# An attention and feed-forward kernel whose order of operations is held as a table

## The chip, the core and the metric

One core of a Trainium2 chip runs the program. Its engines are PE (TensorE, matmuls), DVE (VectorE), ACT (ScalarE), POOL (GpSimd) and SP (SyncE, which here only issues DMAs). Each engine runs its own instructions in their order and waits for the others by semaphores. The metric is the device time of one execution in microseconds (us), lower is better; three runs of the kernel before gave 217.38, 217.80 and 217.99.

## The reference

Attention over four batches of 8 heads, 768 positions and 64 dimensions, in which a position sees the first four positions (the sinks) and the last 128; its output, 3072 rows of 512, goes through a feed-forward layer with 2048 hidden units and a squared relu.

```python
def _attn_ref(q, k, v, n_sink, window):
    B, H, S, D = q.shape                      # 4, 8, 768, 64
    scores = 1.0 / np.sqrt(D) * np.matmul(q, k.transpose(0, 1, 3, 2))
    pos = np.arange(S)
    rel = pos[:, None] - pos[None, :]
    keep = (pos[None, :] < n_sink) | ((rel >= 0) & (rel < window))   # 4, 128
    scores = np.where(keep, scores, -1000000000.0)
    scores = scores - np.max(scores, axis=-1, keepdims=True)
    a = np.exp(scores)
    a = a / (np.sum(a, axis=-1, keepdims=True) + 1e-09)
    return np.matmul(a, v)

def _moe_ref(x, w_in, w_out):                 # x: 3072 x 512, d_ff 2048
    r = np.maximum(x @ w_in, 0.0)
    return (r * r) @ w_out
```

## The kernel before

The kernel builds a list of 825 operations, each a Python closure that emits one or a few instructions, and then runs a planner over the list that fixes the order in which they are emitted and, for operations that more than one engine can do, the engine. As every engine runs what it was given in order, this order is the schedule.

**Work.** For each batch b (0 to 3) and each pair of 128-row blocks s (0 to 2): q and k come in by DMA and are turned so that the head dimension lies on partitions. In batches 0 and 1 PE does it (`transpose`, tile `pt`, L708) and DVE or ACT copy the result out (`unload`, L402, L400); in batches 2 and 3 SP's transposing DMAs do. `scores` (L815, tile `ps`) multiplies two heads at once in two tiles of 64 rows by 128 columns of the array; `sink_scores` (L774, tile `pk`) uses tiles of 128 by 32, and its keys are copied together by `sink_keys` on DVE (L750). All other matmuls use the full 128 by 128. ACT takes the exponential (`expo`, L836), DVE or POOL the mask (`domask`, DVE L845 and L848, POOL L426, two instructions on POOL), PE the product with v (`values`, L884, tile `po`), DVE the division (`norm`, L900 and L901). The result is turned again for the feed-forward layer (`bridge`, L933, with a copy to `xT`, or a transposing DMA).

The first layer (`layer1`, L965, tile `pm`) is 16 matmuls of 256 columns or 8 of 512 for each operation, followed by `relu` (ACT L976 or DVE L978) and `square` (DVE L987 or ACT L985). In batch 3 it is replaced by a scheme with fewer products on sums of blocks (`layer1_fast`): a *quad* has seven products of 4 matmuls of 256 columns or 8 of 128 (L1085, names 1 to 7, in the order 1, 2, 5, 4, 3, 6, 7), and between them DVE takes differences (L1126), ACT or DVE a copy (`first`), a relu (L1141) and DVE a second relu with a sum (`final`, L1153); the squares are L1107 and L1109. Each difference must end before a later product of the quad may write the same half of the bank. Two quads belong to rows 0 to 255 (quads 0,0 and 0,1), four to the rest (1,0 to 1,3).

The second layer (`layer2`, L1174, tile `py`) uses 64 matmuls of 512 columns for two of batch 0's pairs; all other pairs of blocks u use `layer2_fast`: four sums on DVE (`sum`, L1242), seven products of 8 matmuls of 256 columns (L1284, in the order c, d, a, b, c, d, a), evictions between them (`x`, `u`: L400, L402, L1309, L1325, L1332) and the store of 256 rows by 512, 512 KB, from SP (L1359). The very last pair (batch 3, u=2, the `tail`) stores its quarters separately; its last product has 16 matmuls of 128 columns, and its two halves are copied by DVE and by ACT and stored by SP (L1352) and ACT (L1353).

**PSUM.** Two pools of two slots each, `att` and `den`, hold all matmul results. A slot is free again when its last reader is done; an operation that needs a slot waits for that, and so do all behind it on PE.

**The order.** `Plan.run` picks, again and again, the ready operation with the earliest start by assumed costs of each operation on each engine; two numbers for each operation (`SHIFTS`) move its start and its rank. `warm` puts matmuls of the identity into PE's early gaps.

**Names.** An operation's number is its place in the list. Used below: 319 and 325 are first-layer operations of batch 1; 210 the sink scores of batch 1; 341 a relu; 441 the first product of batch 1's second layer and 467 a later one, for which 459 makes a sum on DVE; 446 the eviction `u` of batch 1's pair 0; 407 a mask of batch 2; 616 the first product of pair 0 of batch 2's second layer, 624 and 646 products of its pairs 0 and 1; 683, 685 and 686 the products 5, 4 and 3 of quad 0,0; 743, 721 and 760 products of quads 1,2, 1,0 and 1,3; 779 a product of batch 3's pair 0; 801 the last product of batch 3's pair 1, 802 to 804 its last sum, its first quarter and its 512 KB store; 820 the tail's last product, 822 the copies and stores of its two halves; 39 a load of batch 1's keys.

Of the kernel before, what the change touches and what calls it, by code (L numbers as in the profile page):

```python
# [17 lines left out]
LATENCY = 0.135  # L18
PE_SLACK = 0.0
DMA_START = {"sp": 1.45, "act": 1.2, "pool": 1.6}  # L20
DMA_LATENCY = 0.9
WARM_UNTIL = 34.0
SHIFTS = {
    None: ((-0.254, -0.2), (-0.571, -0.26), (-3.153, 0.8), (-0.345, -0.74), (-0.83, 3.28), (-0.98, -0.76),
        (1.458, 1.69), (-1.232, 0), (0.55, -0.13), (-1.841, -0.16), (-0.527, -1.31), (-1.271, -0.72), (-0.963, 0.32),
        (0.605, -2.77), (-1.323, 1.3), (-1.6, 0.58), (-2.678, -2.44), (-1.476, -0.28), (-2.561, -0.7),
        (-1.331, -0.42), (-1.151, -0.2), (-1.253, -0.22), (-0.398, -0.87), (0.902, 2.55), (-1.318, -0.7),
        (-1.389, -0.4), (-1.246, -0.74), (-0.947, 8.2), (-1.272, 0.2), (-0.428, -2.57), (-1.738, 0), (-1.257, -0.22),
        (-0.151, -1.78), (0.73, -2.69), (-1.258, -0.08), (-1.109, 1), (-1.269, -0.18), (-0.332, -1.95),
        (-1.198, 0.88), (-1.403, -0.28), (-0.085, 0.43), (-1.257, -0.22), (-1.492, -0.14), (-1.966, -0.82),  # L30
        (-1.228, 2.28), (-0.609, -0.3), (-1.172, -0.72), (-0.948, 1.33), (-1.214, -0.14), (-0.818, 0.07),
        (0.509, 0.34), (-1.258, 0.66), (-1.614, 0.1), (-0.282, -0.76), (-0.521, -1.37),),
    ('prep', 0, 0): ((-0.212, 1.23), (-0.072, -0.24), (-0.19, 0.16), (-0.726, 0.34), (0.102, 1.1), (-0.535, 0.02),
        (-0.602, -0.59), (0.354, 0.3), (-3.718, -4.59), (0.634, 0.85), (-0.293, -1.06), (-1.346, -1.52),
        (-0.272, 0.1), (0.418, -0.32), (-0.151, 0.16), (-0.447, -0.7), (0.314, -0.72), (0.319, 0.77), (-0.551, 0.09),
        (-0.072, 0.2), (-0.13, 0.16), (0.105, 0.24), (1.083, 0.83), (0.872, 0.89), (-0.583, 0.42), (-0.732, -0.4),),
    ('sink', 0, 0): ((4.752, 1.43), (1.667, 2.03),),
    ('att', 0, 0): ((0.347, 0.31), (0.954, 0.9), (-0.499, -1.83), (0.762, -2.15), (0.932, -0.05), (-2.305, -7.94),
        (-0.09, 0.64), (-0.608, -0.19),),
    ('val', 0, 0): ((-0.669, 0.31), (-0.697, -0.27), (2.439, -2.91), (-0.554, 0.35), (-0.437, -0.15), (-0.471, 0.35),  # L40
        (-0.386, 0.35), (-0.377, 0.25),),
    ('turn', 0, 0): ((1.726, 0.79), (1.562, 0.69), (1.948, 1.13), (1.496, 0.73),),
    ('att', 0, 1): ((3.244, 0.46), (11.783, 1.08), (3.403, 0.48), (2.622, -0.1), (0.081, -0.49), (-0.044, -0.15),
        (11.287, 1.58), (1.317, -0.32), (2.357, -0.58), (1.537, 1.18), (-0.135, 0.19), (-0.111, -0.81),),
    ('val', 0, 1): ((-1.139, 2.3), (-0.295, 1.56), (-0.887, 1.68), (-0.625, 1.18), (-3.257, -5.22), (-3.374, -3.06),
        (-3.291, -3.92), (-2.551, -2.62),),
    ('turn', 0, 1): ((0.396, -1.51), (-0.815, -0.63), (-0.017, -0.23), (-0.694, 0.15), (-0.252, 1.39),),
    ('prep', 0, 1): ((0.244, -0.3), (0.839, 0.68), (-0.246, 0.32), (0.932, -0.62), (1.027, -0.56), (0.209, -0.32),),
    ('sink', 0, 1): ((1.975, -1.87), (0.782, -1.52),),
    ('att', 0, 2): ((0.244, -0.66), (-1.989, 0.29), (-0.493, 0.33), (0.159, -0.68), (1.032, 0.54), (0.796, 0.57),  # L50
        (-0.189, 0.02), (1.388, -0.12), (0.48, -0.01), (0.313, -0.14), (1.032, 0.72), (-1.933, -0.09),),
    ('val', 0, 2): ((-0.074, -1.39), (-0.782, 0.91), (-0.843, -3.97), (-0.333, 0.47),),
    ('turn', 0, 2): ((0.672, -0.31), (-0.118, -0.09), (0.809, -0.71), (2.596, 0.84),),
    ('l1', 0, 0): ((1.946, 1.98), (2.477, 2.05), (2.842, 0.55), (1.744, 2.15), (1.004, -3.64), (-0.401, 3.09),
        (1.762, -0.33), (2.032, -0.69), (0.818, -0.26), (0.463, 0.08), (2.529, 0.93), (3.08, -0.59),),
    ('l1', 0, 1): ((-1.505, -0.48), (0.385, 0.7), (-1.5, -0.46), (0.416, -0.68), (-0.498, 0.3), (-0.582, 0.6),
        (-0.46, -0.02), (-0.566, -0.1), (0.513, -0.12), (-0.444, -0.02), (-1.914, 1.12), (-0.022, 0.42),),
    ('l1', 0, 2): ((1.159, -0.13), (1.171, -0.31), (4.523, 0.49), (0.77, -0.87), (1.53, -0.41), (0.926, -0.79),
        (0.522, -0.76), (1.124, -0.01), (1.066, -0.47), (4.319, 0.45), (0.749, -2.99), (0.301, -1.88),),
    ('prep', 1, 0): ((-3.284, 0.24), (-1.096, -0.94), (0.605, -0.58), (0.247, -2.12), (-5.483, 0.49), (0.694, 0.02),  # L60
        (0.597, -0.24), (0.597, -0.24), (-8.208, 1.17), (0.681, -1.4), (-1.5, -0.64), (0.357, -0.54), (-10.29, 0.97),
        (0.494, -0.72), (0.633, -0.24), (-0.776, -0.16), (0.529, -0.04), (-1.768, -0.84),),
    ('sink', 1, 0): ((0.868, 0.19), (0.763, 0.03),),
    ('att', 1, 0): ((-0.287, -0.2), (-4.964, -0.65), (-1.435, -0.81), (-3.607, -0.91), (-2.001, -0.01),
        (-0.447, -0.1), (-0.674, 0.1), (-0.719, -0.6), (-0.604, 0.18), (-0.781, -0.2),),
    ('val', 1, 0): ((-6.954, 1.31), (0.072, -4.26), (-0.107, -0.44), (-0.058, -0.46),),
    ('turn', 1, 0): ((-4.522, 0.82), (-0.734, 2.5), (-1.073, 0.44), (0.276, 0.05),),
    ('att', 1, 1): ((1.003, 0.22), (1.223, 0.6), (0.413, -0.45), (0.232, -0.07), (0.259, -0.21), (0.322, -0.07),
        (1.914, -1.56), (0.055, 0.01), (0.085, -2.03), (0.176, 0.47),),
    ('val', 1, 1): ((0.205, 0.29), (-0.249, -0.53), (-2.761, 0.71), (0.377, -0.27),),  # L70
    ('turn', 1, 1): ((0.754, 1.22), (2.068, -0.78), (0.857, 1.68), (-4.788, 1.81),),
    ('prep', 1, 1): ((2.397, 1.96), (5.859, 1.94), (-0.449, 1.75), (1.83, 1.58), (1.97, 1.7), (0.173, -0.21),),
    ('sink', 1, 1): ((0.987, -0.02), (-0.036, -5.62),),
    ('att', 1, 2): ((1.119, -4.28), (0.959, -0.36), (0.499, 1.02), (0.438, -0.34), (1.738, -0.38), (0.767, 0.25),
        (1.547, -0.3), (1.332, 0.31), (1.014, 0.54), (0.269, -2.08),),
    ('val', 1, 2): ((1.128, -0.41), (3.047, 0.37), (3.469, 0.88), (2.416, -3.47),),
    ('turn', 1, 2): ((-4.356, -7.65), (-0.607, -0.19), (-1.006, 0.46), (-4.587, -4.53),),
    ('wt', 0): ((-0.423, 0.42), (-0.315, 0.14), (-1.716, 1), (-0.361, 0.06),),
    ('l2', 0, 0): ((6.071, 1.48), (1.943, -1.23), (2.592, 0.39), (0.401, -1.21), (5.784, 0.74), (5.992, 1.58),
        (2.993, -2.81), (2.732, 0.86), (0.489, -0.39), (-0.516, -1.21), (2.415, 0.45),),  # L80
    ('l2', 0, 1): ((-0.438, 1.25), (-0.215, 0.46), (-0.282, 0.35), (0.307, -0.75), (-0.329, 0.71), (0.749, -0.74),
        (0.871, 0.46), (0.785, 0.08), (0.702, 1.69), (-0.352, 0.8), (2.254, -2.28),),
    ('sum', 0, 2): ((0.045, -1.68), (0.204, -1.02), (-0.718, -2.55), (0.064, -1.38),),
    ('l2', 0, 2): ((0.177, 0.43), (0.08, 0.05), (0.043, -0.01), (0.087, 0.13), (0.146, -0.05), (0.286, 0.01),
        (-3.566, 0.64),),
    ('ev', 0, 2): ((0.387, -2.73), (0.215, -1.01), (-0.063, -1.45), (-0.129, -4.69), (0.419, -1.95), (0.228, -0.91),
        (-0.334, -3.43), (0.529, -0.75),),
    ('l1', 1, 0): ((-2.25, 1.33), (0.301, 1.9), (2.02, -1.38), (0.412, 0.1), (0.164, 0.26), (0.039, -0.22),
        (0.926, -8.17), (-0.524, 0.12), (0.373, 0.12), (1.304, 1.55), (1.015, 0), (0.579, -0.12), (0.204, -0.09),
        (0.523, 0.4), (-0.028, -0.17), (-1.901, 0.85), (0.353, 0.12), (0.196, 0.02), (-1.978, -2.11), (1.417, -0.02),  # L90
        (0.319, -0.99), (0.194, -4.07), (-3.291, 0.39), (0.291, 2.35),),
    ('l1', 1, 2): ((2.497, -0.43), (3.349, 0.01), (2.786, -0.17), (2.851, -0.17), (2.812, 1.03), (0.807, 1.08),
# [109 lines left out]
}  # L202


class Slot:

    def __init__(self, pools, readers):
        self.pools = (pools,) if isinstance(pools, str) else pools  # L210
        self.pool, self.readers, self.end = self.pools[0], readers, 0.0


class Op:
# [6 lines left out]

class Plan:

    def __init__(self, capacity):
# [8 lines left out]
    def place(self, shifts):  # L240

        seen = {}
# [1238 lines left out]
```

## Time and profile before

| | us |
|---|---|
| three runs | 217.38, 217.80, 217.99 (median 217.80) |
| the profiled execution | 217.69 |
| its span, first to last instruction | 216.0 |
| ACT, POOL busy in the span | 123.2, 98.7 |
| granted TensorE clock | 1.00 |

How to read it: a row of the timeline is start, length, engine, line, operation, output and inputs, shape, and how many instructions were merged; in brackets the idle time before it and what ended it. Matmuls overlap in a pipeline and their ends are modelled, so the distance between starts tells more than the lengths. Groups of instructions end in: total busy time, mean ns of one | idle time before them. Some of them, which carry prices below:

```profile
L976 ACT ACTIVATE r<-pm 128x1024 bf16<-128x1024 f32 x30 | 30.7, 1023 | 17.3 <-PE pm L965 15.6 <-DVE gT_sb L987 1.4
L978 DVE TENSOR_SCALAR r<-pm 128x1024 bf16<-128x1024 f32 x6 | 7.3, 1220 | 2.0 <-PE pm L965 2.0
L987 DVE TENSOR_TENSOR gT_sb<-r 128x1024 bf16<-128x1024 bf16 x26 | 19.3, 741 | 17.3 <-ACT r L976 17.1
L848 DVE TENSOR_TENSOR expm<-expm,tri 128x1024 bf16<-128x1024 bf16 x14 | 11.0, 791 | 5.1 <-ACT expm L836 4.9
L426 POOL TENSOR_SCALAR_AFFINE_SELECT expm<-expm 128x512 bf16<-128x512 bf16 x36 | 27.3, 787 | 55.9 <-ACT expm L836 43.7 <-DVE xn_sb L901 12.2
out_dram<-osb SPq DMA_DIRECT2D x11, 512.0 KB, 3.7
```

### The profile page before, as it was taken

How to read it: one execution, taken by the hardware profiler on the slowest of the kernel's cores; microseconds unless marked ns; L12 is line 12 of the kernel's file. 1: busy time of each engine (PE TensorE's matmuls, PEld its weight loads, DVE VectorE, ACT ScalarE, POOL GpSimd, SP SyncE). 2: the span in 40 equal slices, each digit the busy share in tenths (PEclk: the TensorE clock that was granted, in tenths of full speed). 3: DMA queues.
4: the chain of work that ended last, by engine and by line, in shares of the span. 5: the costliest groups of instructions: out<-in, count | busy, mean ns of one | idle time of the engine just before them, and what ended most of it. 6: DMA issues, size and time to landing. Idle time of an engine off the chain costs nothing.

```text
span 216.0 us, 5470 instructions
## 1 busy us (share of the span) xinstructions
PE 206.5 (96%) x2287; PEld 165.4 (77%) x2287; DVE 161.5 (75%) x292; ACT 123.2 (57%) x158; POOL 98.7 (46%) x137
## 2 busy tenths in 40 slices
PE   3999999999999999999999999999999998999993
PEld 3858996689486755688887965598898998897882
DVE  6487458773958569688689994477995859999973
ACT  2498567366663775976757268566623369482100
POOL 7799773698935974898954424002302000000000
PEclk9999999999999999999999999999999999999999
DMA  5999999999997699999999936000023260000133
GB/s 156 261 182 206 174 199 213 160 154 205 156 147 169 88 147 133 167 108 147 142 199 133 139 84 209 3 0 0 3 97 75 52 219 3 2 0 5 55 132 107
DMA packets 93625, 26.09 MB, mean 121 GB/s; under 512 B 86816, under 2 KB 91552, under 8 KB 93600
## 3 DMA queue, kind: packets, MB, share of 16 engines
q0 software_dynamic: 69248, 12.59, 80.3%
q1 hardware_dynamic: 24168, 13.07, 28.1%
q8 instruction: 18, 0.29, 0.6%
q10 hardware_dynamic: 184, 0.07, 0.1%
q14 instruction: 7, 0.06, 0.1%
HBM read 27.30 MB, written 6.29 MB: 156 GB/s over the span
## 4 chain that ended last, share of the span: by engine, by line
PE 73%; DVE 14%; ACT 3%; DMA 3%; issue 3%; SPq 2%; DVEq 0%; ACTq 0%
PE pm L965 29%; PE py L1284 20%; PE po L884 6%; PE py L1174 6%; PE ps L815 5%; PE pm L1085 4%; DMA qr<-in_q_dram 3%; DVE sg L1242 3%; ACT expm L836 2%; DVE t L1126 2%; DVE r L1153 2%; SPq L557 2%; PE px L933 1%; DVE gT_sb L1109 1%; DVE expm L848 1%
## 5 line engine op out<-in xcount | busy, mean ns | idle before, releaser
L965 PE MATMUL pm<-xT,w_in_sb 128*128 128x256 bf16 (+1 forms) x448 | 66.1, 304 | 0.0
L965 PEld LDWEIGHTS <-w_in_sb 128*128 128x128 bf16 x448 | 48.3, 114 | 13.4 <-issue 1.3
L836 ACT ACTIVATE expm<-ps 128x1024 bf16<-128x1024 f32 (+1 forms) x48 | 43.7, 951 | 18.1 <-PE ps L815 17.5
L426 POOL TENSOR_SCALAR_AFFINE_SELECT expm<-expm 128x512 bf16<-128x512 bf16 x36 | 27.3, 787 | 55.9 <-ACT expm L836 43.7
L976 ACT ACTIVATE r<-pm 128x1024 bf16<-128x1024 f32 x30 | 30.7, 1023 | 17.3 <-PE pm L965 15.6
L1284 PEld LDWEIGHTS <-gT_sb 128*128 128x128 bf16 x336 | 31.2, 98 | 4.3 <-issue 0.7
L987 DVE TENSOR_TENSOR gT_sb<-r 128x1024 bf16<-128x1024 bf16 x26 | 19.3, 741 | 17.3 <-ACT r L976 17.1
L1284 PEld LDWEIGHTS <-sg 128*128 128x128 bf16 x240 | 22.4, 98 | 4.5 <-DVE sg L1242 1.0
L1284 PE MATMUL py<-wt,sg 128*128 128x256 bf16 x160 | 20.8, 273 | 0.4 <-DVE sg L1242 0.4
L1284 PE MATMUL py<-wt,gT_sb 128*128 128x256 bf16 x160 | 20.8, 273 | 0.0
L1284 PE MATMUL py<-w_out_sb,gT_sb 128*128 128x256 bf16 x144 | 18.5, 273 | 0.0
L884 PEld LDWEIGHTS <-expm 128*128 128x128 bf16 x352 | 16.3, 97 | 2.5 <-issue 0.7
L901 DVE TENSOR_TENSOR xn_sb<-po,rc 128x512 bf16<-128x512 f32 (+1 forms) x28 | 17.2, 615 | 1.0
L884 PE MATMUL po<-v,expm 128*128 128x65 bf16 x352 | 17.5, 193 | 0.3 <-DVE xT L402 0.2
L1174 PE MATMUL py<-w_out_sb,gT_sb 128*128 128x512 bf16 x64 | 15.3, 380 | 0.0
L848 DVE TENSOR_TENSOR expm<-expm,tri 128x1024 bf16<-128x1024 bf16 x14 | 11.0, 791 | 5.1 <-ACT expm L836 4.9
L815 PE MATMUL ps<-qkT 64*128 64x256 bf16 (+1 forms) x256 | 14.6, 238 | 0.0
L815 PEld LDWEIGHTS <-qkT 64*128 64x128 bf16 x256 | 8.1, 94 | 7.1 <-issue 6.1
L884 PE MATMUL po<-vs,es 128*128 128x65 bf16 x128 | 12.9, 193 | 0.0
L400 ACT ACTIVATE osb<-py 128x256 f32<-128x256 f32 (+1 forms) x15 | 6.6, 441 | 10.2 <-PE py L1284 7.1
L884 PEld LDWEIGHTS <-es 128*128 128x128 bf16 x128 | 11.7, 97 | 0.0
L587 POOL DMA_DIRECT2D v<-in_v_dram x12 | 11.0, 927 | 0.2
(97 smaller groups left out, 330.5 us busy)
## 6 DMA issues: line engine op xcount, KB each, us to landing
out_dram<-osb SPq DMA_DIRECT2D x11, 512.0 KB, 3.7
v<-in_v_dram POOLq DMA_DIRECT2D x24, 128.0 KB, 7.5
qn<-in_k_dram POOLq DMA_DIRECT2D x20, 128.0 KB, 7.5
qn<-in_q_dram POOLq DMA_DIRECT2D x20, 128.0 KB, 7.4
w_in_sb<-in_moe_w_in_dram POOLq DMA_DIRECT2D x4, 512.0 KB, 10.3
w_out_sb<-in_moe_w_out_dram POOLq DMA_DIRECT2D x4, 512.0 KB, 10.2
qr<-in_k_dram SPq DMA_DIRECT2D x4, 256.0 KB, 5.7
qr<-in_q_dram SPq DMA_DIRECT2D x4, 256.0 KB, 5.3
```

The lines of the kernel that those rows point to most:

```text
L426: nc.gpsimd.affine_select(out=e_tile, in_=e_tile, compare_op=ALU.is_ge, fill=fill, base=i - 1, pattern=[[0, n], [1 if i else -1, 128]], ch ...
L587: return [nc.gpsimd.dma_start(out=v_sb[b % 2][:, t, :, 0:D], in_=v[b, :, 128 * t:128 * t + 128, :].rearrange("h p d -> p h d"))]
L815: nc.tensor.matmul(ps[:, h2, o:o + w], lhsT=qkT_sb[r, m, 1, c, :], rhs=qkT_sb[r, m, 0, qb:qb + w // 128, :], start=(i == 0 and not biased) ...
L836: nc.scalar.activation(out=x[:, :, o:512], in_=bank_t["s", b, s, m][:, :, o:512], func=AF.Exp, scale=scale)
L848: nc.vector.tensor_mul(y, y, tri.rearrange("p (o a) c -> p o (a c)", o=1).to_broadcast([128, 4, 256]))
L884: touch(("po", b, s, m0), e, nc.tensor.matmul(pv[:, i, h2, :], lhsT=lhsT, rhs=rhs, start=(n_ == 0), stop=(n_ == len(mms) - 1)), j)
L901: touch(("po", b, s, m0), e, nc.vector.tensor_tensor(out=xn_sb[:, 2 * s:2 * s + 2, 128 * (m0 + j0):128 * (m0 + j0 + nj)].rearrange("p i (j ...
L965: nc.tensor.matmul(pm[:, i, :], lhsT=w_in_sb[:, fb // 4, kb, fb % 4:512:4], rhs=xT[:, c0 // 256:(c0 + cw) // 256, kb, :], start=(kb == 0), ...
L976: nc.scalar.activation(out=o, in_=h, func=AF.Relu)
L987: nc.vector.tensor_mul(g, r, r)
L1174: touch((b, u), e, nc.tensor.matmul(pm[:, i, :], lhsT=gT_sb[:, fb, 128 * t:128 * t + 128], rhs=w_out_sb[:, fb, :], start=(fb == 0), stop=( ...
L1284: ins = nc.tensor.matmul(y_, lhsT=x[:, i, :], rhs=r_, start=(first or tail and n == 2) and i == 0, stop=i == HB - 1, skip_group_check=not ...
```

## The change

The planner, its costs and the table `SHIFTS` go. A table `ORDER` lists the 825 operations in the order in which they are emitted. A letter behind a number names the engine where there is a choice (p, d, a, g for PE, DVE, ACT, POOL), and `+0` or `+1` which PSUM pool a slot is taken from. `DUMMIES` gives the number of identity matmuls before an operation. The operations are the same; 91 of them are on another engine than before.

```diff
-LATENCY = 0.135
-PE_SLACK = 0.0
...
-SHIFTS = {
...
+ORDER = """
...
+168 171 169d 159 172a 173d 160a 170a 165 131 177 166d 167d 178d 132a 133a 161a 144 146 145 148 174 128 289 149d 130d
...
+396 399 397 322 254+1 255 263+0+0 264 333a 339d 323d 324d 258g 371 372 260g 265d 340 261+0 398 262 341a 266 267d 319
...
+526a 640a 621a 520a 609 615 641 634 639 620 679+1 680 693+1 623 695a 694 697 642 681d 650 622 643 676 683 682 685
+624 651 696 698 677 625 678 646 644 594 595 610 611 684 686 699 687a 700 627 645 647 626 648d 652 689 690 701a 703
+654 691 628 707 692d 629a 704 655 739+0 657 740 688a 649 710 705 708 653 656a 741a 743 725+1 711+1 706a 702a 713a
+727a 659a 742 744 709 712 726 658 661 729 714 767 715 717 745 660 663 664 662 665 716 728 730 769 731 732 666 667d
...
+808 781 811a 810 812 813 816 783 787 815 817 784a 785 788 789 814d 790 791 792d 818 819 824 793 796 794 797 795d 821
+823 798 799 800 801 802 820 822 803a 804
+"""
+DUMMIES = {
+    57: 26, 63: 18, 64: 3, 83: 3, 91: 3, 97: 5, 101: 3, 119: 2,
 }
...
     def run(self):
-        free = {p: [0.0] * n for p, n in self.capacity.items()}
...
-                cand = (round(pick[1] + o.lag, 2), o.key)
-                if best is None or cand < best[0]:
-                    best = (cand, o, pick)
...
+        free = dict(self.capacity)
+        names = {"p": "pe", "d": "dve", "a": "act", "g": "pool"}
+        words = ORDER.split()
+        assert len(words) == len(self.ops)
+        for word in words:
+            word, *chosen = word.split("+")
+            n = int(word.rstrip("pdag"))
+            o = self.ops[n]
+            assert o.engine is None and all(a.engine for a in o.after + o.follow), n
+            o.engine = names[word[-1]] if word[-1] in names else next(iter(o.engines))
             for s in o.takes:
-                free[s.pool].sort()
-                free[s.pool].pop(0)
...
+                if len(s.pools) > 1:
+                    s.pool = s.pools[int(chosen.pop(0))]
+                assert free[s.pool], (n, s.pool)
+                free[s.pool] -= 1
+            self.idle = DUMMIES.get(n, 0)
+            o.run(o.engine)
             for s in o.reads:
                 s.readers -= 1
-                s.end = max(s.end, end)
                 if not s.readers:
-                    free[s.pool].append(s.end)
...
+                    free[s.pool] += 1
...
     def warm(dst, key=None, h=0):
-        if P.now < WARM_UNTIL:
-            for _ in range(min(26, int(0.5 * P.gap / 0.056))):
...
+        for _ in range(P.idle):
+            ins = nc.tensor.matmul(dst, lhsT=ident, rhs=ident, start=True, stop=True,
+                                   is_transpose=dst.dtype == BF16)
...
-    P.place(SHIFTS)
     P.run()
```

## The prediction, made before the changed kernel was run

> **What bounds the kernel now.** The page first: which engine is full, and what the chain that ended last runs through.
>
> ```profile
> PE 206.5 (96%) x2287; PEld 165.4 (77%) x2287; DVE 161.5 (75%) x292; ACT 123.2 (57%) x158; POOL 98.7 (46%) x137
> PE 73%; DVE 14%; ACT 3%; DMA 3%; issue 3%; SPq 2%; DVEq 0%; ACTq 0%
> ```
>
> PE is busy nearly always, so a new order of the same matmuls can only win where PE loses time inside that busy share. To find it I read the timeline of PE by starts, not by ends: with nothing in the way a matmul of 256 columns starts 109 ns after the last, one of 128 after 56, of 65 after 29, of 512 after 216. Whatever exceeds that is lost.
>
> ```profile
> 60.35 1.04 PE L1284 MATMUL py<-w_out_sb,gT_sb 128*128 128x256 bf16 x8
> 61.32 0.61 PE L815 MATMUL ps<-qkT 64*128 64x128 bf16 x12
> 61.87 1.05 PE L1284 MATMUL py<-wt,sg 128*128 128x256 bf16 x8
> ```
>
> Eight steps of 109 ns are 0.87 us, but the scores start 0.97 us after the product: 0.10 us for the change of tile from 128 to 64 rows; leaving costs about 0.09 more (148 ns for a 56 ns step). PE changes its tile shape 64 times, so 64 x 0.10 = 6.5 us go there. The other losses are waits:
>
> ```profile
> 176.67 0.61 PE L1085 MATMUL pm<-xs,w_in_sb 128*128 128x128 bf16 x8 [0.18 <-DVE t L1126]
> 178.39 1.05 PE L1085 MATMUL pm<-xs,wi 128*128 128x128 bf16 x16 [0.22 <-ACT r L1141]
> 179.93 1.06 PE L1085 MATMUL pm<-xs,qkT 128*128 128x256 bf16 x8 [0.48 <-DVE xs L1043]
> ...
> 199.81 0.61 PE L1284 MATMUL py<-wt,sg 128*128 128x256 bf16 x4 [0.38 <-DVE sg L1242]
> ```
>
> Here batch 3's fast first layer runs alone on PE while its sums and differences queue on DVE. By starts, PE loses 2.6 us between 172 and 193, 0.54 at 199.8 and 0.19 at 208.8; between 17 and 172 only 1.5 us in eight places. Together 4.8 us: all that a better order can take from waits.
>
> The windows view says who is full there:
>
> ```profile
> 172.00:193.00 21.00, 19.79 (x226) 18.69 (x224) 17.81 (x28) 14.34 (x18) 0.00 (x0) 1.00 0.19 63
> 193.00:200.00 7.00, 6.62 (x61) 5.72 (x60) 6.76 (x10) 2.94 (x5) 0.00 (x0) 1.00 0.01 4
> ```
>
> The columns are length, PE, PEld, DVE, ACT, POOL, clock: DVE is full from 193 to 200 (6.76 of 7.00), ACT is not. The clock is 1.00 throughout, so it is no lever.
>
> Last, the end, from the timeline:
>
> ```profile
> 208.41 0.38 SPq L1359 DMA_DIRECT2D out_dram<-osb  x1
> ...
> 212.48 0.28 ACT L400 ACTIVATE half<-ya 128x128 f32<-128x128 f32 x1 [3.32 <-PE ya L1284]
> 212.78 0.35 ACTq L1353 DMA_DIRECT2D out_dram<-half  x1
> 213.22 0.40 SPq L1352 DMA_DIRECT2D out_dram<-osb  x1
> ```
>
> The last matmul ends at 212.4, call it E. The 512 KB store of batch 3's second pair goes out at 208.41, well before; only quarters follow. The last, 64 KB at 213.22, lands 1.8 us later by the DMA view, and 0.95 us of closing work ends the span at 216.0 = E + 3.6.
>
> **The change, part by part.**
>
> *Planner gone, table in.* Host work; no instruction. The first 32 PE operations stand as before and the dummy matmuls are the same counts, so the start (to about 25 us) is priced at nothing; what follows keeps PE as its cover.
>
> *Shape changes.* I wrote PE's 260 operations out in both orders: blocks of scores or sink scores change the shape 64 times before, 63 after. One change fewer: -0.1 us. What the change says of tile shapes is done, and is worth almost nothing.
>
> *Engines.* 91 operations change engine. Up-projection relu: 13 to DVE, 4 back, 9 x 1.220 = +11.0 us of DVE; its squares: 7 to, 11 back, -4 x 0.741 = -3.0; masks: 7 from POOL, 3 back, +4 x 0.791 = +3.2; narrow evictions net 5 x 0.42 = +2.1; two 512-wide ones +1.3; batch 3's relu, spread and copy 1.22 + 0.74 + 0.64 = +2.6; its squares net -0.7; turns' copies -1.4. Sum +15.0 us on DVE (161.5 to about 176, 82% of the span); ACT loses 7.9, POOL 6.3. The cover is PE's own time: from the first layer-2 product of batch 1 (441) on, PE has 107 us of rows, DVE 107 by the mean durations and 102 by start-to-start steps (a DVE 0.69 follows the last after 0.61); before it was 97 by the means. Hidden, but with little left.
>
> *A rule against this.* Beside a POOL mask, DVE steps stretch:
>
> ```profile
> 147.67 0.98 DVE L1242 TENSOR_TENSOR sg<-gT_sb 128x1024 bf16<-128x1024 bf16 x1
> 148.69 0.69 DVE L1242 TENSOR_TENSOR gT_sb<-gT_sb 128x1024 bf16<-128x1024 bf16 x1
> ```
>
> POOL masks at 146.89 to 148.11, and the step beside it takes 0.98 for 0.69. The Trainium skill, "SBUF — State Buffer", section "Who interferes with whom", says that a DVE instruction with two SBUF inputs and a GpSimd one that reads SBUF exclude each other for a whole instruction. By that rule each of the 28 mask instructions left on POOL (36 before) could hold DVE for its whole 0.787 us, 22 us at worst. By the row it is 0.3 each, and only where they meet. My sum uses the row's means, which hold it.
>
> *PE's order in the middle (32 to 164).* I laid the operations out with the rows' durations: PE at its steps (product 0.87, sixteen 256-wide matmuls 1.75, scores 0.55 + 0.10, values 0.72), each relu, mask or norm behind its matmul in its engine's own order, each PSUM slot free when its last reader ends. PE then waits at few places. Sink scores of batch 1 (210): their keys stand behind a relu on DVE, 0.25. Up-projection 319 needs a "den" slot; the relu (341) that frees it stands behind a square on ACT, 0.5. Product 467 needs the sum 459, eighteenth in an unbroken row of DVE steps since 446 (11.0 us from 30.2 against PE at 40.9), 0.35. Some ten more are just in time or 0.1 late. Sum 1.8, against 1.5 before: no gain here.
>
> *Layer 2 of batch 2 spread through batch 3's first layer.* Quads 0,0 and 0,1 now start 13 PE places earlier, and thirteen products of 0.87 us stand between quad products that wait for each other. Example: 686 needs the difference of 683; before, nothing but quad products stood between. Now 624 and 646 do, 2 x 0.87 us, against a difference of 0.69 and its queue. Laid out the same way, about 0.7 us of waits remain from 616 on (743 behind ACT's queue 0.2, 721 0.25, 760 and 779 about 0.1 each) against 3.3 before: -2.6.
>
> *DMAs and queues.* POOL issues the same loads in the same order. A sink-values step (1.75 us) moves in front of 39, but these loads already sit behind landings ("POOL qn L578 <- DMA w_out_sb" waits 5.3 us), so it costs nothing. Batch 3's fourteen loads now go ahead of three masks: 14 x 0.9 = 12.6 us, and mask 407 is needed 9 us after. Of SP, the transposes change places among themselves and have 4 us or more to spare.
>
> *The end.* The order of batch 3's pairs is now 0, 2, 1, with pair 2's last quarter at the very end. So the 512 KB store (804) is last. Its first quarter (803) is moved to ACT, behind 822 in ACT's order, and 822 waits for the last matmul: 0.28 copy and 0.35 issue, then 0.38 for 803, so 804 goes out at about E + 1.1 where the last 64 KB went at E + 0.8. It moves 512 KB: the store of 208.41 ran at 254 to 264 GB/s from 209 to 211, done 2.7 us after its issue; the page's median is 3.7. I take 2.8: E + 3.9, and 0.95 to close gives E + 4.9 for E + 3.6: +1.3 us (bounds +0.9 and +2.2).
>
> *Sum.* -0.1 + 0.3 - 2.6 + 1.3 = -1.1 us against the profiled 217.69: 216.6. The runs' median, 217.8, lies 0.1 above that execution: **216.7**, which I forecast. The bounds: waits from 616 on may all go (-3.3) or stay (0), the middle may cost nothing (-1.5) or 2 us more than laid out.
>
> **The rivals.**
>
> *DVE becomes the bound (slower).* From 441 on DVE has 102 us of steps and PE 107 + 2; I count some 3 us in which DVE must itself wait for PE. That leaves 4 us. If DVE's steps take their full means there (107), 5% more, each unbroken row of some 11 us like that before 467 ends 0.55 us later; five such rows make 2.7 us more waiting, of which I take 2.5: 216.7 + 2.5 = 219.2. For it: DVE is the engine that ends PE's waits now, and gets 10 us more. Against: before, its steps did overlap. It decides the case from 4 us of lost DVE time on, where no slack is left.
>
> *The end eats the gain.* Half of the 2.6 us comes, 1.3 are paid at the end: 217.8, no change. For it: ten places with under 0.2 us of slack.
>
> *All waits go.* 4.8 - 0.5 saved, 1.0 paid at the end: -3.4, 214.4. Against: PE would have to be late nowhere.
>
> **How the numbers follow.** Forecast -1.1: 0.5, and its own range 215.9 to 217.4. DVE bound 0.26, no change 0.12, all waits gone 0.12. A measurement of this kernel tells 0.3% from no change, 0.65 us. Faster: nearly all of the forecast (0.43; its slow edge counts as same) and the last case 0.12, 0.55. Same: 0.18. Slower: 0.27. The range takes in part of both edges: 215.2 to 219.2.
>
> **What would show it.** PE's waits between 172 and 200 down from 3.1 us to under 1, with layer-2 rows of batch 2 between the quads'. DVE near 176 us. The last 512 KB store issued about 1 us after the last matmul and the span ending near E + 4.9. If the span ends at E + 3.6, my price of the end is wrong; if PE waits on DVE or ACT rows in many places between 95 and 170, the forecast falls to the first rival.

## The result: slower by 0.8%, and the profile after

The changed kernel takes 219.52 us (median of 13 runs) against 217.81 for the one before in the same session: a ratio of 1.0084, 95% interval 1.0061 to 1.0108. The forecast was 216.7, range 215.2 to 219.2: wrong in sign, and 0.3 us outside the range. The profiled execution took 219.54 with a span of 217.7 (before: 217.69 and 216.0), so the span grew by 1.75 us. All traces below are of executions within 1 us of their kernel's median except that of e11_norms, a slow one 2.7 us above it, which is used for the order of events and not for the kernel's time.

First the page of the changed kernel: engines, the chain of waits by engine, then groups (the line numbers are those of the changed file: relu 762 and 764, square 773, masks 634 and 212) and the large stores.

```profile
PE 204.7 (94%) x2287; PEld 164.5 (76%) x2287; DVE 172.0 (79%) x307; ACT 113.6 (52%) x147; POOL 94.8 (44%) x129
PE 78%; DVE 14%; issue 2%; DMA 2%; POOL 1%; ACT 1%; SPq 1%; ACTq 0%; DVEq 0%; POOLq 0%
L764 DVE TENSOR_SCALAR r<-pm 128x1024 bf16<-128x1024 f32 x15 | 18.3, 1222 | 11.2 <-PE pm L751 8.9
L773 DVE TENSOR_TENSOR gT_sb<-r 128x1024 bf16<-128x1024 bf16 x22 | 16.5, 757 | 4.5 <-ACT r L762 4.4
L212 POOL TENSOR_SCALAR_AFFINE_SELECT expm<-expm 128x512 bf16<-128x512 bf16 x28 | 22.6, 833 | 51.8 <-ACT expm L622 47.2
out_dram<-osb SPq DMA_DIRECT2D x11, 512.0 KB, 2.8
```

DVE's busy time gained 10.5 us and ACT's lost 9.6. PE still is busy 94% of the span (before 96%); the chain's share of DVE stands at 14% as before. The page does not show where the time went. The windows view does: length, then busy time (and count) of PE, PEld, DVE, ACT, POOL, and the clock. After:

```profile
97.00:127.00 30.00, 28.00 (x349) 23.55 (x347) 26.92 (x51) 14.06 (x19) 10.38 (x13) 1.00 1.26 116
127.00:150.00 23.00, 21.27 (x184) 13.19 (x184) 18.67 (x26) 12.35 (x13) 5.81 (x7) 1.00 0.30 48
...
172.00:193.00 21.00, 21.00 (x219) 20.21 (x217) 19.57 (x33) 12.11 (x17) 0.00 (x0) 1.00 0.19 77
193.00:200.00 7.00, 7.00 (x66) 6.38 (x65) 6.84 (x11) 4.15 (x6) 0.00 (x0) 1.00 0.01 2
```

The same view of the kernel before, for the first two of these stretches:

```profile
97.00:127.00 30.00, 29.91 (x366) 25.05 (x365) 25.94 (x45) 17.52 (x24) 17.61 (x21) 1.00 1.85 144
127.00:150.00 23.00, 23.00 (x171) 15.44 (x170) 15.05 (x21) 15.64 (x18) 5.39 (x6) 1.00 0.21 62
```

From 172 to 200 PE is now full (28.00 of 28.00, before 26.41): the gain that was forecast is there. From 97 to 150 it stood full before (52.91 of 53) and now lacks 3.7 us. By the starts of PE's matmuls, counting only losses over 0.08 us and taking 0.10 off where the tile shape changes:

| stretch of the span, us | waits before | waits after |
|---|---|---|
| 17 to 97 | 0.78 | 0.13 |
| 97 to 172 | 0.61 | 5.08 |
| 172 to the last matmul | 3.24 | 0 |
| last matmul to the end of the span | 3.55 | 5.18 |

PE's own end hardly moves (212.44 before, 212.56 after); the end of the span moves by the 1.6 us of the last row. So there are two losses to explain, 4.5 us in the middle and 1.6 at the end, against 3.9 won. (The first 17 us differ from one traced execution to the next: the first up-projection starts at 16.96 in after, at 17.30 in before and as late as 18.25 in an experiment. So traces are compared here by their waits, and kernels by the medians of their runs.) The waits view names what stands behind the middle ones (engine, line, what it waited for, total, times, longest):

```profile
PE pm L751 <- DVE r L764: 1.4, 1, 1.4
PE pm L751 <- DMA xT<-xn_sb: 1.1, 1, 1.1
PE po L670 <- DVE xn_sb L687: 0.9, 2, 0.7
PE po L670 <- ACT u L186: 0.5, 1, 0.5
PE ps L601 <- DVE xn_sb L687: 0.4, 1, 0.4
```

Six single places, behind three different engines and queues. In the order of operations they are: scores 428 at 100.9 (0.44 by starts beyond the change of shape), values 433 and 426 at 113.6 and 115.5 (0.87 and 0.33: their PSUM slots are freed by the divisions 418 and 411), up-projection 497 at 127.35 (1.27: the transposes 404 and 420), up-projection 521 at 146.0 (1.54: the slot that relu 501 frees), values 608 at 161.6 (0.64). The first of them comes and goes: in the traces of kernels with the same order up to there it is between 0 and 0.68, and no experiment is about it.

The end, from the timeline of the changed kernel:

```profile
211.50 1.06 PE L1070 MATMUL ya<-w_out_sb,gT_sb 128*128 128x128 bf16 x16
...
212.90 0.35 ACTq L1139 DMA_DIRECT2D out_dram<-half  x1
213.63 0.38 ACT L186 ACTIVATE osb<-py 128x256 f32<-128x256 f32 x1 [0.76 <-ACT half L186]
214.04 0.38 SPq L1145 DMA_DIRECT2D out_dram<-osb  x1
```

The 512 KB store goes out at 214.04, 1.5 us after the last matmul (E + 1.1 was forecast), lands 2.79 us later, and 0.9 us of closing work ends the span.

### The profile page after: what moved, and what is told of

It is laid out like the page before. It is cut to its first block, busy times and chain, and to the rows that moved or that the text cites. A ratio compares the mean times of both kernels' runs of the same rounds, so it can differ in the third digit from the quotient of the medians.

```text
span 217.7 us, 5452 instructions
## 1 busy us (share of the span) xinstructions
PE 204.7 (94%) x2287; PEld 164.5 (76%) x2287; DVE 172.0 (79%) x307; ACT 113.6 (52%) x147; POOL 94.8 (44%) x129
## 4 chain that ended last, share of the span: by engine, by line
PE 78%; DVE 14%; issue 2%; DMA 2%; POOL 1%; ACT 1%; SPq 1%; ACTq 0%; DVEq 0%; POOLq 0%
PE pm L751 25%; PE py L1070 22%; PE pm L871 9%; PE py L960 5%; PE po L670 5%; PE ps L601 5%; DVE gT_sb L773 3%; PE pt L494 2%; DVE r L764 2%; PE pt L179 2%; DMA xT<-xn_sb 2%; DVE sg L1028 2%; PE px L719 1%; DVE qkT L795 1%; DVE expm L634 1%
## 5 line engine op out<-in xcount | busy, mean ns | idle before, releaser
L751 PE MATMUL pm<-xT,w_in_sb 128*128 128x256 bf16 (+1 forms) x448 | 67.1, 304 | 2.5 <-DVE r L764 1.4
L751 PEld LDWEIGHTS <-w_in_sb 128*128 128x128 bf16 x448 | 47.8, 114 | 16.0 <-issue 4.8
L212 POOL TENSOR_SCALAR_AFFINE_SELECT expm<-expm 128x512 bf16<-128x512 bf16 x28 | 22.6, 833 | 51.8 <-ACT expm L622 47.2
L762 ACT ACTIVATE r<-pm 128x1024 bf16<-128x1024 f32 x21 | 21.3, 1023 | 19.6 <-PE pm L751 12.9
L764 DVE TENSOR_SCALAR r<-pm 128x1024 bf16<-128x1024 f32 x15 | 18.3, 1222 | 11.2 <-PE pm L751 8.9
L773 DVE TENSOR_TENSOR gT_sb<-r 128x1024 bf16<-128x1024 bf16 x22 | 16.5, 757 | 4.5 <-ACT r L762 4.4
L634 DVE TENSOR_TENSOR expm<-expm,tri 128x1024 bf16<-128x1024 bf16 x18 | 13.1, 727 | 2.7 <-ACT expm L622 2.6
L186 ACT ACTIVATE osb<-py 128x256 f32<-128x256 f32 (+1 forms) x13 | 5.3, 417 | 18.7 <-PE py L960 5.8
L771 ACT ACTIVATE gT_sb<-r 128x1024 bf16<-128x1024 bf16 x14 | 14.7, 1056 | 0.2
L601 PE MATMUL ps<-qkT 64*128 64x128 bf16 (+1 forms) x256 | 14.4, 238 | 0.4 <-DVE xn_sb L687 0.4
```

The source lines that it names most:

```text
L212: nc.gpsimd.affine_select(out=e_tile, in_=e_tile, compare_op=ALU.is_ge, fill=fill, base=i - 1, pattern=[[0, n], [1 if i else -1, 128]], ch ...
L601: nc.tensor.matmul(ps[:, h2, o:o + w], lhsT=qkT_sb[r, m, 1, c, :], rhs=qkT_sb[r, m, 0, qb:qb + w // 128, :], start=(i == 0 and not biased) ...
L751: nc.tensor.matmul(pm[:, i, :], lhsT=w_in_sb[:, fb // 4, kb, fb % 4:512:4], rhs=xT[:, c0 // 256:(c0 + cw) // 256, kb, :], start=(kb == 0), ...
L762: nc.scalar.activation(out=o, in_=h, func=AF.Relu)
L764: nc.vector.tensor_scalar_max(o, h, 0.0)
L773: nc.vector.tensor_mul(g, r, r)
```

## The experiments

Every kernel below is the changed one with words of its table `ORDER` moved or their letters changed, or with tables joined; nothing is left out of the computation. Fragments of the table are shown without its line breaks. "Against after" is the difference of the two ratios to the kernel before, times 217.8; half the width of an interval is some 0.3 to 0.7 us, so a difference of two runs of this table is known to some 0.6 to 0.9: those of e1, e4 and e6 are not clear of nothing by their times alone, and there the traces have to speak. Line numbers in these kernels are those of after or one less.

| run | what is moved | median us | ratio to before, 95% | against after, us |
|---|---|---|---|---|
| after | | 219.52 | 1.0084 [1.0061, 1.0108] | |
| e1_end | 512 KB store ahead of the last copies | 219.81 | 1.0098 [1.0079, 1.0117] | +0.3 |
| e2_before_to_490 | before's front, after's rear | 217.25 | 0.9976 [0.9962, 0.9990] | -2.4 |
| e3_after_to_490 | after's front, before's rear | 223.38 | 1.0247 [1.0216, 1.0279] | +3.6 |
| e4_sp | two transposes on SP | 219.27 | 1.0062 [1.0048, 1.0076] | -0.5 |
| e5_end_before | before's end | 218.27 | 1.0030 [1.0012, 1.0049] | -1.2 |
| e6_670 | sum 670 later | 219.09 | 1.0072 [1.0046, 1.0099] | -0.3 |
| e7_454 | quarter 454 earlier on ACT | 218.85 | 1.0044 [1.0028, 1.0061] | -0.9 |
| e8_both | before's front and end, after between | 216.02 | 0.9915 [0.9895, 0.9936] | -3.7 |
| e9_670_early | sum 670 earlier | 218.80 | 1.0038 [1.0019, 1.0056] | -1.0 |
| e10_591 | mask 591 from POOL to DVE | 218.41 | 1.0042 [1.0022, 1.0061] | -0.9 |
| e11_norms | divisions earlier on DVE | 220.94 | 1.0134 [1.0112, 1.0156] | +1.1 |
| e12_all | four repairs together | 215.02 | 0.9873 [0.9849, 0.9896] | -4.6 |
| e13_norms_454 | e11 and e7 | 218.09 | 1.0020 [1.0000, 1.0039] | -1.4 |
| e14_best | e12 and mask 605 earlier | 214.58 | 0.9861 [0.9838, 0.9884] | -4.9 |

### The end: e1_end and e5_end_before

```diff
-798 799 800 801 802 820 822 803a 804
+798 799 800 801 802 803a 804 820 822
```

> After's order with one change at the very end: the first quarter and the 512 KB store of batch 3's second pair (803 on ACT, 804) stand ahead of the tail's last product and its copies and stores (820, 822). Theory: in the trace of after ACT copies and issues the tail's half first, so 804 goes out at 214.04, 1.5 us after the last matmul; now 802 ends at 212.4, 803 takes 0.38, 804 goes out near 212.8 and lands 2.8 later, 0.95 to close: the span falls by 1.2 us, time 218.3. Rival: the 512 KB transfer shares its end with the tail's four quarters and is hidden by nothing earlier, the queue on ACT does not matter: at most -0.3, 219.2.

The store went out 1.1 us earlier, as expected, and nothing was won. Timeline of e1_end:

```profile
212.93 0.38 SPq L1144 DMA_DIRECT2D out_dram<-osb  x1
213.17 0.35 ACTq L1138 DMA_DIRECT2D out_dram<-half  x1
213.41 0.42 SPq L1137 DMA_DIRECT2D out_dram<-osb  x1
```

By the trace the 512 KB landed at 216.16, and the two 64 KB stores that now stand behind it at 216.47 and 216.81, 3.3 and 3.4 us after their issue, where the same two took 1.6 in after. The span ended at 217.73, to a hundredth where it ended in after. So ACT's queue, which the prediction had made the cause, was not it: the last landing comes at 216.8 in either order. (By the DMA packets the last bytes had moved at 216.18 in e1 and at 216.45 in after; what holds e1's last landing back until 216.81 no run shows.) e5 therefore keeps the large transfer away from the end altogether, with before's order of the last two pairs from 782 on (its core shown):

```diff
-779 782 766d 786 805 780 806 809 807 808 781 811a 810 812 813 816 783 787 815 817
+779 782 766a 786 787 788 789 780 781 783 784d 785 790 792a 791 793 795a 794 797 796 798 801
...
-798 799 800 801 802 820 822 803a 804
+799 800 802 803d 804 811d 815 813 816 818 819 824 817 821 823 820 822
```

> After's order up to the last product of batch 3's pair 0 (782), then before's: pair 1 before pair 2, so the 512 KB store goes out some 4 us before the last matmul. Advancing that store by 1.1 us alone moved nothing, because then the tail's 64 KB stores stand behind its packets (3.4 us to land instead of 1.6). Theory: the price of the end is that a 512 KB transfer begins within 3 us of the last matmul at all; taken back, the span ends at the last matmul + 3.55 again, -1.6, and before's waits of 0.5 and 0.2 in these pairs come back: 219.5 - 0.9 = 218.6. Rival: the four quarters and the closing work set the end whatever goes before them: 219.5 + 0.7 = 220.2.

-1.2 us, near the theory's -0.9 and not the rival's +0.7. Timeline of e5_end_before:

```profile
208.88 0.38 SPq L1144 DMA_DIRECT2D out_dram<-osb  x1
```

The 512 KB store is issued 4.3 us before the last matmul ends (213.18), and the span ends 3.5 us after the last matmul again (216.70). The waits that before had in these pairs did not come back.

### Front and rear: e2_before_to_490, e3_after_to_490, e8_both

The list of before's planner (with its engines and slots) up to product 490, then the changed table without the words already used; e3 is the mirror, and e8 is e2 with before's order from 782 on.

```diff
-ORDER, all of it
+before's order up to 490, then ORDER without these words
```

> Before's order and engines up to product 490 (batch 1's second layer, PE at about 127 us), after's order and engines for all that is left, its end too. Theory (the three parts add up): late part -3.2, end +1.6, and of after's waits behind 490 the one on the transposes (1.27 at 497) goes, those at 521 (1.54) and 608 (0.64) stay, against 0.24 that before has there: 217.8 - 3.2 + 1.6 + 1.9 = 218.1. Rival: the waits at 521 and 608 are only the late echo of what DVE and SP lost before 490; then they go too: 216.2.

> The mirror of the last one: after's order and engines up to product 490, before's for all that is left, with before's end. Theory: 0.5 us more waits up to 490 (0.54 + 0.87 + 0.33 + 0.15 against about 1.4), 1.27 at 497 because SP's transposes are still queued behind others, then before's own late waits: 217.8 + 0.5 + 1.3 = 219.6. Rival: after's front costs nothing by itself and the loss arises only from its own rear: 217.9.

> Before's order up to product 490, after's from there to 782, before's end (pair 1 before pair 2). Theory: it keeps what after gains in batch 3's first layer (PE ends 2.1 us earlier than before in the run with after's end) and drops the end's price: 217.25 - 0.9 = 216.3, faster than both kernels. Rival: the late gain and the end hang together (DVE is late for pair 1's sums without pair 2 in between), 217.5.

e2 gave 217.25, between the theory's 218.1 and the rival's 216.2: the wait of 1.54 at 521 was gone too, as in before's front the sum 670 has been made long before. In the place of the wait on the transposes stands one of 0.74 at 126.6, put down to a copy on DVE. From 172 on PE lost nothing: the late gain comes with after's rear, whatever the front. e8 gave 216.02, as the theory said, and is faster than both kernels. e3 missed by 3.8 us: it was to be 219.6 and was 223.38. After's front hands over more debts than its own waits show. Timeline of e3_after_to_490, then its windows (PE's clock is the last but two):

```profile
128.39 0.34 PE L600 MATMUL ps<-qkT 64*128 64x128 bf16 x4 [1.94 <-DMA qkT<-qn]
130.29 0.45 PE L600 MATMUL ps<-qkT 64*128 64x128 bf16 x8 [1.57 <-DMA qkT<-qn]
```

```profile
130.70:131.20 0.50, 0.50 (x5) 0.30 (x4) 0.00 (x0) 0.50 (x1) 0.00 (x0) 1.00 0.18 36
131.20:134.85 3.65, 3.65 (x11) 1.31 (x10) 3.23 (x3) 2.33 (x4) 2.27 (x2) 0.53 0.53 108
```

Before's rear has batch 3's scores 580 right behind product 490, where after's has 3.6 us of up-projections between. They need the transposes 552 to 555, and 553 stands last of the four in SP's row, issued at 127.6 by the view of the tile `qkT`: waits of 2.1 and 1.6 us by starts, for the 1.27 that the same late row costs in after: +2.4. On top, the granted clock then averaged 0.53 over 3.65 us, worth 3.65 x 0.47 = 1.7. Together that is the miss of 3.8 and a little more. The lower clock does not come every time: of the six runs two have a mean clock of 1.00, and they took 221.97 and 222.65.

### The transposes: e4_sp and e7_454

Timeline of SP in after; each transpose takes 1.2 to 1.9 us of its queue:

```profile
115.28 0.33 SPq L1145 DMA_DIRECT2D out_dram<-osb  x1
115.70 1.59 SPq L448 DMA_TRANSPOSE qkT<-qn  x1
117.39 1.85 SPq L701 DMA_TRANSPOSE xT<-xn_sb  x1
119.34 2.64 SPq L448 DMA_TRANSPOSE qkT<-qn  x2
122.03 3.16 SPq L701 DMA_TRANSPOSE xT<-xn_sb  x2
```

The last row is 404 and 420. The division that 404 needs had ended at 100.8; it stands behind the store 455 and four transposes, and in the kernel before that store went out 5.7 us earlier:

```profile
109.58 0.33 SPq L1359 DMA_DIRECT2D out_dram<-osb  x1
```

Timeline of ACT, of after:

```profile
114.60 0.38 ACT L186 ACTIVATE u<-py 128x256 f32<-128x256 f32 x1 [4.35 <-DVE osb L1095]
114.88 0.38 ACT L186 ACTIVATE osb<-py 128x256 f32<-128x256 f32 x1
```

The second row is 454, the quarter that the store carries. It could have run at 111.2, when DVE's 453 ended, but is queued behind 465, and 465 comes behind DVE's 466, which reads the same bank. A table that counts waits within one engine sees two ACT operations in a row; the store and the transposes behind them are on another engine.

```diff
-471 472 478 482 571 574 572 483 486 485 564 419 555 554 404 420 556 553
+471 472 478 482 571 574 572 483 486 485 564 419 404 420 555 554 556 553
```

> After with one change on SP's queue: the two transposes of batch 2's attention output that up-projection 497 needs (404, 420) stand ahead of two transposes of batch 3's q and k (555, 554) that took SP from 119.34 to 122.03. Theory: they go out 2.7 us earlier, the wait of 1.27 us on PE at 127.35 goes, time 218.3. Rival: DVE's row behind it runs on its own time, so what PE gains at 127 it waits at 146 (1.54 there becomes 2.8): 219.5, unchanged.

```diff
-388 432d 345d 451 453 475
+388 432d 345d 451 453 454a 475
...
-403 463 410 476 466 411 465a 454a 551
+403 463 410 476 466 411 465a 551
```

> After with one ACT step moved: the quarter 454 of batch 1's pair 0 stands behind 453, ahead of 465, instead of behind it. In after 465 waits for DVE's 466 until 114.56, so 454 runs at 114.88 and the 512 KB store 455, which heads SP's queue, goes out at 115.28, and seven transposes of 1.3 us each stand behind it. Theory: 454 runs at about 111.3, the store goes out at 111.7, the transposes 404 and 420 land 2 us earlier, and the wait of 1.27 at 127.35 goes: -1.2, 218.3. Rival: SP is held next by transpose 419, which needs norm 411 (115.4), so little is won: -0.4, 219.1.

e4 took away over half of the wait, from 1.27 to 0.49 by the trace, and nothing came back behind it (1.55 at 521, as in after); its -0.5 us alone would not show it. e7 took the wait to 0.11, and its -0.9 us is clear. SP in e7_454:

```profile
112.38 0.33 SPq L1144 DMA_DIRECT2D out_dram<-osb  x1
...
120.05 2.67 SPq L700 DMA_TRANSPOSE xT<-xn_sb  x2
```

The wait at 497 thus comes, but for 0.1 us, from one ACT operation in the wrong place, some 15 us earlier and two engines away.

### Sum 670 and the masks on POOL: e6_670, e9_670_early, e10_591

DVE's and POOL's rows of after around PE's longest wait, from the timeline:

```profile
140.94 2.60 DVE L795 TENSOR_TENSOR qkT<-w_in_sb 128x2048 bf16<-128x2048 bf16 x1
141.22 1.23 POOL L212 TENSOR_SCALAR_AFFINE_SELECT expm<-expm 128x512 bf16<-128x512 bf16 x2
143.46 1.11 DVE L773 TENSOR_TENSOR gT_sb<-r 128x1024 bf16<-128x1024 bf16 x1
144.68 1.22 DVE L764 TENSOR_SCALAR r<-pm 128x1024 bf16<-128x1024 f32 x1
145.96 3.22 PE L751 MATMUL pm<-xT,w_in_sb 128*128 128x256 bf16 x28 [1.37 <-DVE r L764]
```

The first is 670, a sum of 2048 columns that takes 1.21 where nothing is beside it; the fourth is relu 501, for whose slot PE waits. Three edits, each alone:

```diff
-587 500 510d 584d 670 511d 590 562 563 588 515 501d 508d 585
+587 500 510d 584d 511d 590 562 563 588 515 501d 508d 670 585
```

> After with one DVE step moved: the sum of w_in 670 (2048 wide, 2.60 us beside the POOL masks at 141.22 and 143.27, where 672, the same shape, took 1.21) stands behind the square 508 instead of ahead of relu 501, for whose PSUM slot PE waits 1.54 us at 145.96. Theory: the wait goes, -1.4, 218.1, and 670 takes near 1.2 where no POOL mask runs beside it. Rival (DVE is the bound, 82% full): what is moved is only put later, PE waits the same 1.2 for the norms and squares behind it, 219.3.

```diff
-497 512 565 669 573 498a 513d
+497 512 565 669 573 670 498a 513d
```

> After with the sum of w_in 670 moved the other way: ahead of relu 513, into the 2.1 us that DVE stands idle before 131.01 in after's trace. Moved later, it had only shifted PE's wait (1.54 at 146 gone, 1.14 at 149.6 new). Theory: DVE is full only in the row from 135 to 150, not over the kernel; work taken out of that row and put into an idle gap wins what PE waits there: wait at 146 gone and none at 149.6, -1.5, 218.0. Rival (DVE has no slack anywhere there; what it does at 129 it lacks at 135): 219.3.

```diff
-547 591g 589g 596
+547 591d 589g 596
```

> After with one mask, 591, taken from POOL and put on DVE at its place in the order, where it is the 28th DVE instruction behind 670. Theory (a POOL mask and a DVE step with two inputs in SBUF hold each other up): 670, 2.60 us beside POOL's 141.22 to 142.45, falls to 1.22, relu 501 ends 1.4 earlier, PE's wait at 146 falls from 1.54 to about 0.2, though DVE does 0.7 us more later: -1.0 to -1.3, 218.3. Rival (670 is slow for another reason, its 2048-wide read of w_in): 670 stays at 2.6, the wait stays, 219.6.

e6: the wait of 1.54 went, and one of 1.04 beyond the change of shape came at 149.6; -0.3, near the rival's number. And the stretch did not go with 670: it passed to the square 511 that now stood in its place. DVE in e6_670:

```profile
140.85 2.08 DVE L772 TENSOR_TENSOR gT_sb<-r 128x1024 bf16<-128x1024 bf16 x1
...
144.88 1.21 DVE L794 TENSOR_TENSOR qkT<-w_in_sb 128x2048 bf16<-128x2048 bf16 x1
```

e9: -1.0, between the theory (-1.5) and the rival (-0.2); the trace, in which both waits are gone, speaks for the theory. DVE is nearly full from 135 to 150 in after (14.00 of 15.00 us) and idle for 2.1 us just ahead of it, so a step taken back over that border is won, and one pushed forward is not. e10: with the mask off POOL, 670 takes 1.22 and PE's wait is 0.05, -0.9, though DVE does more. DVE in e10_591:

```profile
142.27 1.22 DVE L794 TENSOR_TENSOR qkT<-w_in_sb 128x2048 bf16<-128x2048 bf16 x1
143.41 0.69 DVE L772 TENSOR_TENSOR gT_sb<-r 128x1024 bf16<-128x1024 bf16 x1
```

The difference, 1.38 us, is the time of POOL's two mask instructions (1.23) and a little more, as if DVE stood still for both. The Trainium skill, "SBUF — State Buffer", section "Who interferes with whom", says that a DVE instruction with two inputs in SBUF contends with a GpSimd one that reads SBUF, over ports that form an exclusive lock; the measurement agrees, and adds the price.

### The divisions, and all repairs together: e11_norms, e13_norms_454, e12_all, e14_best

```diff
-451 453 475 430d 417 418
+451 453 417 418 430d 475
...
-463 410 476 466 411 465a 454a
+463 410 411 466 465a 454a
...
-426 459 434
+426 459 476 434
```

> After with DVE's row from 111 to 116 in another order: the divisions 418 and 411, whose PSUM slots the products with v (433, 426) wait for, ahead of mask 430 and sum 475, and of 466 and 476; the sum 476 goes behind 459. Theory: the waits at 113.61 (0.87) and 115.55 (0.33) shrink to 0.4 together, 418.7 is out of the question for the sum of both, so -0.8, 218.7, if what follows has 1 us of slack. Rival: the wait at 127.35 on SP's transposes takes it back (PE comes to 497 0.8 us earlier, the transposes do not): 219.4.

(The figure 418.7 in it is a slip of the pen and stands for nothing.) The waits at 113.6 and 115.5 fell from 1.20 to 0.55 together, and the kernel got 1.1 us slower. The trace shows the place: DVE's 466, which 465 and behind it 454 wait for, now stands behind division 411 and ends some 0.5 us later, counted from the first up-projection; store 455 goes out as much later, and the transposes 404 and 420 some 0.7 and 2.3. PE waits at 497:

```profile
129.78 5.30 PE L750 MATMUL pm<-xT,w_in_sb 128*128 128x512 bf16 x16 [2.67 <-DMA xT<-xn_sb]
```

Is the edit bad, or does it only pay once SP's queue is free? e13 joins it with e7's:

> After with two of the repairs: the divisions' order (which alone gave 220.9) and quarter 454 ahead of 465 on ACT (which alone gave 218.85). Theory: the order of the divisions lets PE come to 497 earlier, which is worth nothing while the transposes come later; with the store out at 111.7 the transposes are in time, and both waits go: 218.85 - 0.8 = 218.0. Rival: the new order of DVE's row is bad in itself (sum 476 and mask 430 later), 219.5 or more.

218.09 against 218.0: the second. Alone +1.1; with 454 repaired no loss, and perhaps a gain (-0.5 on top of e7's -0.9, which is within the intervals). e12 joins e11, e7, e9 and e5; e14 adds one step, mask 605:

```diff
-614 674d 675 616 618d 617 619 601 605d 602
+614 605d 674d 675 616 618d 617 619 601 602
```

> After with four repairs together: the divisions' order of the last run, quarter 454 ahead of 465 on ACT, 670 in DVE's gap at 129, and before's end (pair 1 before pair 2). Theory (after's loss is these places and no more): waits of 1.2 - 0.4, 1.27, 1.54 and the end's 1.25 go, 219.5 - 0.8 - 1.2 - 1.5 - 1.25 = 214.8, under the 216.0 of before's front with after's rear. Rival: DVE, busy 172 of 217 us, makes up new waits for half of it: 217.

> The four repairs together (215.0) and a fifth: mask 605 on DVE stands ahead of 674, 675 and 618 instead of behind them. PE's last wait of the middle, 0.65 at product 608, ends 0.06 after 605 ends by the trace, though it is put down to an ACT instruction that the order emits later. Theory: 605 is what 608 waits for; 1.3 us earlier the wait goes, -0.6, 214.4. Rival: ACT's evictions 621 and 640 are what it waits for: 215.0.

e12: 215.02 against the theory's 214.8. Its page:

```profile
PE 204.2 (96%) x2282; PEld 164.5 (77%) x2287; DVE 170.6 (80%) x306; ACT 114.9 (54%) x148; POOL 93.5 (44%) x129
PE 84%; DVE 7%; DMA 3%; SPq 2%; issue 1%; ACT 1%; DVEq 0%; ACTq 0%
```

DVE's work is after's, to 1.4 us, its share of the chain is halved, and the kernel is 4.6 us faster than after and 1.3% faster than before. e14 gave 214.58 (214.4 expected; 0.4 less than e12, which is within the intervals), and in its trace the wait at 608 is gone: the trace had put it down to ACT's `u`, which the order emits behind 608, and it was DVE's mask 605. e14_best has the lowest median of all, 0.9861 of before (0.9838 to 0.9884); it and e12 cannot be told apart by their times.

## Why the prediction was wrong, step by step

**What bounds the kernel now.** Right as far as it went: PE's waits were the only thing to win, and 172 to 200 the place. It did not ask what kept the middle at 0.6 us of waits.

**Planner gone, shape changes.** Right: 63 changes for 64, and some 6 us over their steps in both kernels. (64 x 0.10 is 6.4 and not 6.5; nothing rests on it.) One change fewer was worth nothing that shows.

**Engines.** The durations of DVE's instructions add up to 14.9 us more (187.1 for 172.2), as forecast. Its busy time grew by 10.5 only, to 172.0 and not to 176: each step's record begins a little before the last one's ends, so that the 161.5 to which the prediction added 15 was not a sum of durations. Hidden in sum, as said: e12 runs in 215.0 with it.

**A rule against this.** The rule was weighed and set aside for the row of 0.3 us. In after about a dozen two-input DVE steps are stretched by over 0.1 us, some 6 us together (before: as many, 4 to 5 us), far from the 22 of its worst case; but one of them by 1.38, in a row that PE waits behind. The error was to price the mean and not to ask which steps meet: 0.9 us (e10).

**PE's order in the middle.** This is the step that failed: "Sum 1.8, against 1.5 before: no gain here." Measured 5.2 from 17 to 172. The three places it named (210, 319, 467) cost 0.13 together at most; the six that cost were put at nothing. It laid out PE against DVE, ACT and slots with mean durations, which misses the stretched 670 (1.54 at 521) and the chain over ACT and SP (1.27 at 497), and it does not name the divisions 418 and 411, which are 0.87 and 0.33 late.

**DMAs and queues.** Failed with it: "the transposes change places among themselves and have 4 us or more to spare". Their head, store 455, was not looked at; it went out 5.7 us later, and the spare was -1.27 (e7: 0.11 with the store early). Of POOL it counted fourteen loads ahead of the masks and not the two behind them (544 goes out at 114.67, before at 108.13); no run showed a cost of that.

**Layer 2 of batch 2 through batch 3's first layer.** The mechanism was right, the size too small: -3.2 for -2.6; no wait over 0.08 us is left. e2 and e8 show it to be independent of the front.

**The end.** +1.6 for +1.3, within its bounds. Of its terms the transfer (2.8) and the closing work (0.95) were right, the issue came at E + 1.5 and not E + 1.1. The cause was half right: not ACT's queue (e1: nothing), but a 512 KB transfer that starts after E at all (e5: -1.2).

**The rivals.** "DVE becomes the bound" gave 219.2, near the 219.5 measured, and the prediction's sign for it, many waits on DVE rows between 95 and 170, is there: of the 5.1 us in the middle 3.8 wait for DVE steps, in five places, and 1.3 for SP's queue. But its reason, DVE's sum, was not the cause: with 170.6 us of DVE e12 runs in 215.0, and e10 wins by giving DVE more. It was the order of DVE's steps, and the one that POOL stretched; that the number came so near is partly luck. What holds of it is its word on unbroken rows: e6 shows that a step pushed back within 135 to 150 is paid for there. "All waits go" came true from 172 on alone, and "the end eats the gain" had the end right and not the middle.

## What to carry to other kernels

A new order must be laid out on every engine and queue, the DMA issuers too: for each transfer ask what heads its queue, and follow that back over the engines, because one copy in the wrong place on an idle engine (ACT, 52% busy) cost 1.3 us 15 us later on another. Try repairs together as well as alone: one that cost 1.1 us by itself cost nothing once the next wait behind it was gone. Keep the last large store well ahead of the last matmul, not merely ahead of the small ones: 4.3 us before its end was early enough here, 0.3 us after it was not, and no run lies between.

## What the runs showed of the hardware

- A DVE step with two inputs in SBUF can be stretched by the time of two POOL masks in a row and a little more: 2.60 us for 1.22 (670) and 2.08 for 0.69 (511), in whichever of them stands there; a relu with one input from PSUM takes 1.23 beside two POOL masks (e6, 143.04), 1.22 without.
- PE's granted clock averaged 0.53 over 3.65 us after waits of 1.94 and 1.57 us with 0.3 us of work between them (e3, in the traced execution); after one of 1.37 (after) it stayed at 1.00. In e3 that added 1.7 us to what the waits themselves cost.
- Two 64 KB stores issued just behind one of 512 KB took 3.3 and 3.4 us to land, for 1.6 ahead of it.
